# LN2 of the first two token blocks cut into single tiles, the table load moved to the start, and a new written order, in an adaLN + H3 convolution + SwiGLU kernel

## The chip, the cores and the metric

The kernel runs on one core of a Trainium2 chip. The time is the device time of one execution in microseconds (us). The kernel before takes 597.68 us, the median of three runs (597.65 to 598.74). A profiled execution of the same kernel took 598.64 us, with a span of 596.9 us in the trace; the rows quoted below are from that one. Engines: PE is the matmul engine (TensorE) and PEld its weight loads, DVE is VectorE, ACT is ScalarE, POOL is GpSimd, SP is the engine whose queue issues the transfers (DMA).

## The reference

```python
mod = (silu(c) @ w_mod).reshape(1, 6, 1, 512)     # sa, ca, ga, sb, cb, gb
h = layernorm(x) * (1 + ca) + sa                  # x: 2048 tokens x 512
k_shift = sum(shift(k, t) * shift_k[:, t])        # 4 taps, causal, per channel
kv = k_shift * v
y = irfft(rfft(kv, 4096) * rfft(ssm_k, 4096))[:2048] + kv * ssm_D
x = x + ga * (h * y)
h = layernorm(x) * (1 + cb) + sb                  # LN2
x = x + gb * ((silu(h @ w_gate) * (h @ w_up)) @ w_down)   # 512 -> 1792 -> 512
```

All of it is in fp32.

## The kernel before, in words

**The front** computes the convolution. The 512 channels are four blocks of 128, numbered 0 to 3 (c_ in the code). For each block the four taps (tap0, tap, L188 to 208) and the product with v (times_v, L211) run on DVE, ACT and POOL in the channel-major layout. The long convolution is a transform in two stages, written as matmuls: x_turn transposes kv on PE, x_first (L233) does the first stage of kv, k_first and k_turn (L253, L271) that of the filter ssm_k; skip (L1045) adds ssm_D to one row of the filter first. swap_x is a stream transpose in place on DVE. The second stage works on half blocks n = 0 to 7 (n // 2 is the block): x3 (L350) makes two of three linear forms of X on PE and copies them out (tile xs), x_sum adds these for the third, product3 (L359) multiplies with the filter's form straight from PSUM (pk) on DVE, and inv3 (L363) turns the three products back on PE, with copies into X on ACT. X0, X1 and X2 are then written to memory (put, tile away) and read back transposed in four transfers (get); X3 is transposed by DVE straight from PSUM (inv3s, L372).

**The gate and LN1.** The 2048 tokens are four blocks t of 512 (128 partitions times 4 token groups i). do_stats, gate_n (L521) and gate_p (L532, two tensor operations per token group with the broadcast modulation bcs) make the factor s that multiplies the convolution's result; each call says on which engine. y_pe (L539) does the last inverse step on PE from the X of two channel blocks, and y_into (L557) multiplies by s, adds to x and takes the statistics for LN2; y_gate and add_y (L551, L567) do the same in two steps. The modulation itself comes from three loads of w_mod (tile wm): mod_mul on ACT, mod_part on POOL or DVE, mod_bc and mod_T on PE, mod_mix on DVE.

**LN2 and the FFN.** The FFN is computed with fp32 split into a high and a low part, three matmuls for one product (PASSES, L774). Token blocks 0 and 1 are the first pair. For each of them: statistics and the power −0.5 on POOL (stats, L444, tile rsb), normalisation of the four token groups (norm2b, L578, tile n, alternating ACT and DVE), transposition into four channel tiles b on PE (norm_t, L594, tile nt, by halves h of two tiles), scale and shift on ACT (norm_s, L602, tile hraw), and the split of a half into high part by ACT (op_hi, L644) and low part by DVE or POOL (op_lo, L651). These are the operands B11, B21 (block 0) and B12, B22 (block 1). The gate and up products of the first two of 14 column blocks f are plain (gu_pe, L849, tile g); from f = 2 on, seven products in place of eight are used (gate_up_first, L911, whose first product is tile a; then gate_up), and the down products (tile dn) are fed in between. That part runs to the end and is the longest.

**What sets the order.** All engines are wrapped (InOrder, L32 to 40), so each one's instructions stand in the order in which the program's text calls them, and every row of the trace has line 40. The text of the front, from load_kh on, is a list of such calls in an order written out by hand. The table SLOTS (L54) gives the buffer for each allocation of five kinds of tile in turn: e8, r4, b16 and k2 in SBUF and ps, four double banks of PSUM. A tile that takes a buffer waits until the last reader of the former one is done. SP issues transfers in its own order too, so a load whose buffer is not free holds up those behind it. warm (L123) and warm_wide (L130) are matmuls without use to the result that are put where PE would wait.

Of the kernel before, what the change touches and what calls it, by code (L numbers as in the profile page):

```python
# [43 lines left out]
def adaln_h3_swiglu(ctx, tc, q, kT, vT, small, ssm, dskip, wgu, wdn, wmod, e_fwd, e_inv, w_c, out):  # L44
# [10 lines left out]
        "e8": "201345670143567013504312312341324314324314324314372154273124572134275124",  # L55
        "ps": "0123012301230123012310231023102310231023102310231023102310231231230123023102310231023102312031203120312031203120312031220310130101023122213021",
        "r4": "0123410231420312130413201401231230124012341023402130423014320413201432041342102314301204134210",
        "b16": "011234514354405234",
        "k2": "012102102010212010212010212010212010212010212021012021012021012021012021012021012021",
# [70 lines left out]
    def warm_wide():  # L130

        t = fp.tile([P, 2, 512], F32, tag="xs", name="wide", bufs=2)
        dve.memset(t, 1.0)
        t = t.bitcast(F32R)
        o = banks("wide")
        for _ in range(6):
            pe.matmul(o[:, 0], t[:, 0, 0:P], t[:, 1], start=True, stop=True)
        for w in (512, 256):
            for _ in range(8):
                for a in range(2):  # L140
                    pe.matmul(o[:, a, 0:w], t[rows(a), 0, 0:P], t[rows(a), 1, 0:w], start=True, stop=True)
# [8 lines left out]
    dve.memset(mhalf, -0.5)  # L150

# [14 lines left out]
    def load_small():  # L166
        sp.dma_start(sm, small)
# [276 lines left out]
    def stats(xs, name, done=False, rows_=range(TB)):  # L444
# [13 lines left out]
        if name in ("b0", "b1"):  # L458
            dve.tensor_scalar(rs[:, 0, :], v, EPS, None, op0=ALU.add)
            pool.tensor_tensor(rs[:, 0, :], rs[:, 0, :], mhalf, op=ALU.pow)  # L460
            dve.scalar_tensor_tensor(rs[:, 1, :], m, -1.0, rs[:, 0, :], op0=ALU.mult, op1=ALU.mult)
            return rs
# [139 lines left out]
    def norm_s(t, h):  # L602

        if not raw_h:
            raw_h.append(b16("hraw", (P, 2, NB, 512)))
        for k, pt in enumerate(NT.pop((t, h))):
            b = 2 * h + k
            act.activation(
                raw_h[0][:, t % 2, b], pt, AF.Identity, scale=modT[:, 1, b : b + 1], bias=modT[:, 0, b : b + 1]
            )  # L610
# [238 lines left out]
    def gu_pe(f, t, h):  # L849

        if h == 0:
            GU[f, t] = two("g")
        for b in (2 * h, 2 * h + 1):
            x = BOP[f"B{b // 2 + 1}{t + 1}"]
            for u in range(2):
                for n, (wa, xa) in enumerate(PASSES):
                    pe.matmul(
                        GU[f, t][u], WG[f][:, wa, u, b, :], x[:, xa, b % 2],
                        start=(b == n == 0), stop=(b == NB - 1 and n == 2),
                    )  # L860
# [169 lines left out]
    csil = cp.tile([P, 8], F32, name="csil")  # L1030
# [40 lines left out]
    def do_norm2a(t):  # L1071
        rs[t] = norm2a(t, True)
# [3 lines left out]

    load_kh(0, 0)
    load_small()
    tap0h(0, 0, e=dve)
    warm(16)  # L1080
    warm_wide()
    load_kh(0, 1)
    load_e(2)
    tap0h(0, 1, e=act)
    taph(0, 1, 0)
    load_ssm(0, 0)
    warm(3)
    load_dskip()
    load_ssm(0, 2)
    taph(0, 1, 1)  # L1090
    tap(0, 2)
    load_v(0)
    tap(0, 3)
    load_e(1)
    load_ssm(0, 1)
    skip(0)
    load_k(1)
    times_v(0, 3, e=dve)
    k_first(0, 2, e=act)
    k_first(0, 1, e=act)  # L1100
    times_v(0, 2, e=dve)
    x_turn(0, 1, e=act)
    times_v(0, 0, e=dve)
    times_v(0, 1, e=dve)
    x_turn(0, 0, e=act)
    load_ssm(0, 3)
    load_e(3)
    k_first(0, 3, e=act)
    load_e(0)
    x_first(0, 0, e=act)  # L1110
    k_first(0, 0, e=act)
    tap0(1, e=dve)
    tap(1, 1)
    tap(1, 2)
    tap(1, 3)
    load_ssm(1)
    skip(1)
    x_first(0, 1, e=act)
    swap_x(1)
    k_turn(0, 0, e=act)  # L1120
    k_turn(0, 3, e=act)
    load_wc()
    load_v(1)
    times_v(1, 1, e=pool)
    k_turn(0, 1, e=act)
    swap_x(3)
    load_k(2)
    load_ssm(2)
    k_first(1, 3, e=dve)
    tap0(2, e=act)  # L1130
    times_v(1, 0, e=pool)
    times_v(1, 2, e=pool)
    k_turn(0, 2, e=act)
    x_turn(1, 0, e=act)
    tap(2, 1)
    swap_x(0)
    load_v(2)
    tap(2, 2)
    k_first(1, 0, e=act)
    k_first(1, 1, e=act)  # L1140
    k_first(1, 2, e=act)
    room()
    skip(2)
    times_v(1, 3, e=pool)
    x_turn(1, 1, e=act)
    swap_x(2)
    silu_c()
    tap(2, 3)
    times_v(2, 1, e=pool)
    times_v(2, 2, e=pool)  # L1150
    x_first(1, 0, e=act)
    x_first(1, 1, e=act)
    swap_x(6)
    swap_x(7)
    x3(0, 2, e=act)
    k_turn(1, 0, e=act)
    x3(0, 1, e=act)
    load_x(2)
    times_v(2, 0, e=pool)
    x3(1, 2, e=act)  # L1160
    x3(1, 1, e=act)
    k_turn(1, 2, e=act)
    k_turn(1, 3, e=dve)
    do_stats(2, 0)
    load_x(1)
    x_sum(0, e=pool)
    mod_load(0)
    mod_mul(0, 1, e=act)
    mod_part(0, 1, e=pool)
    k_turn(1, 1, e=act)  # L1170
    k_first(2, 0, e=act)
    k_first(2, 2, e=act)
    x_sum(1, e=pool)
    k_first(2, 3, e=act)
    swap_x(4)
    x_turn(2, 0, e=act)
    product3(0, 0)
    product3(0, 1)
    product3(0, 2)
    mod_load(1)  # L1180
    mod_mul(0, 0, e=act)
    times_v(2, 3, e=pool)
    product3(1, 2)
    load_k(3)
    load_v(3)
    tap0(3, e=act)
    mod_part(0, 0, e=pool)
    product3(1, 1)
    do_stats(1, 0)
    inv3(0, e=act)  # L1190
    product3(1, 0)
    mod_mul(1, 1, e=act)
    x_turn(2, 1, e=act)
    x3(3, 2, e=act)
    mod_part(0, 2, e=pool)
    inv3(1, e=act)
    tap(3, 1)
    mod_part(0, 3, e=dve)
    tap(3, 2)
    tap(3, 3)  # L1200
    times_v(3, 3, e=pool)
    swap_x(5)
    x_first(2, 0, e=act)
    x_first(2, 1, e=act)
    swap_x(10)
    times_v(3, 0, e=pool)
    load_x(0)
    load_x(3)
    load_w(0)
    mod_part(1, 1, e=pool)  # L1210
    k_first(2, 1, e=act)
    x3(3, 1, e=act)
    do_stats(0, 0)
    swap_x(11)
    x_sum(3, e=pool)
    put(0)
    product3(3, 0)
    x3(2, 2, e=act)
    x3(2, 1, e=act)
    k_turn(2, 0, e=act)  # L1220
    k_turn(2, 2, e=act)
    k_turn(2, 3, e=act)
    x_sum(2, e=pool)
    product3(3, 1)
    times_v(3, 2, e=pool)
    times_v(3, 1, e=pool)
    product3(2, 0)
    product3(2, 2)
    w8_hi(0)
    product3(2, 1)  # L1230
    w8_lo(0, e=pool)
    mod_mul(1, 0, e=act)
    do_stats(3, 0)
    mod_part(1, 0, e=pool)
    mod_part(1, 2, e=pool)
    product3(3, 2)
    mod_part(1, 3, e=pool)
    do_stats(3, 1)
    k_turn(2, 1, e=act)
    x3(5, 1, e=act)  # L1240
    inv3(2, e=act)
    inv3(3, e=act)
    swap_x(9)
    do_stats(0, 1)
    load_ssm(3)
    skip(3)
    x_turn(3, 0, e=act)
    do_stats(1, 1)
    x_turn(3, 1, e=act)
    do_stats(2, 1)  # L1250
    swap_x(8)
    mod_bc(1)
    mod_bc(0)
    mod_mix()
    gate_n(2, 0, e=dve)
    x_first(3, 0, e=act)
    x_first(3, 1, e=act)
    swap_x(14)
    k_first(3, 1, e=act)
    get(0)  # L1260
    k_first(3, 2, e=act)
    k_first(3, 3, e=act)
    k_first(3, 0, e=act)
    x3(5, 2, e=dve)
    x_sum(5, e=dve)
    x3(4, 2, e=act)
    gate_p(2, 0, 1, e=pool)
    gate_p(2, 1, 1, e=pool)
    x3(4, 1, e=act)
    x_sum(4, e=pool)  # L1270
    gate_n(0, 0, e=act)
    gate_n(3, 0, e=act)
    put(1)
    product3(5, 0)
    product3(5, 2)
    gate_p(3, 0, 1, e=pool)
    product3(5, 1)
    load_einv()
    product3(4, 2)
    gate_n(0, 1, e=act)  # L1280
    gate_n(2, 1, e=act)
    gate_n(1, 0, e=act)
    product3(4, 0)
    product3(4, 1)
    get(1)
    inv3(5, e=act)
    inv3(4, e=act)
    swap_x(13)
    k_turn(3, 0, e=act)
    k_turn(3, 3, e=act)  # L1290
    swap_x(15)
    put(2)
    gate_p(3, 1, 1, e=pool)
    k_turn(3, 2, e=act)
    mod_load(2)
    gate_p(0, 0, 1, e=pool)
    gate_p(0, 3, 1, e=pool)
    k_turn(3, 1, e=act)
    x3(7, 2, e=act)
    swap_x(12)  # L1300
    get(2)
    x3(7, 1, e=act)
    gate_p(0, 1, 1, e=dve)
    x3(6, 1, e=act)
    gate_p(1, 0, 1, e=dve)
    gate_p(1, 1, 1, e=dve)
    x_sum(7, e=dve)
    x3(6, 2, e=act)
    product3(7, 1)
    gate_n(3, 1, e=act)  # L1310
    gate_n(1, 1, e=act)
    product3(7, 2)
    x_sum(6, e=pool)
    product3(7, 0)
    gate_p(0, 2, 1, e=pool)
# [276 lines left out]
```

## Time and profile before

| | us |
|---|---|
| median of three runs | 597.68 (597.65 to 598.74) |
| the profiled execution | 598.64 |
| its span in the trace | 596.9 |
| PE busy in the span | 578.0 (97%) |
| DVE busy | 464.3 (78%) |
| ACT busy | 305.4 (51%) |
| POOL busy | 304.1 (51%) |
| first plain product g starts | 165.43 |
| first of the seven products, a, starts | 195.78 |

The rows of the page and of the views are shown with the prediction. A row of a timeline gives the start, the length and the engine of a group of instructions, then output and inputs; in brackets stands the idle time ahead of it and what ended it. A row of a group gives the busy time, the mean in ns of one instruction, and idle time with what ended it.

### The profile page before, as it was taken

To read this page: it belongs to the slowest core of one execution; us is meant where nothing else is said; L and a number is where in the kernel's file an instruction comes from. 1 tells how busy PE (TensorE), PEld (TensorE's weight loads), DVE (VectorE), ACT (ScalarE), POOL (GpSimd) and SP (SyncE) were. 2 spreads that over 40 slices of the span, in tenths; PEclk is the share of its full clock that TensorE was granted. 3 is DMA by queue.
4 is the path that set the end of the run, shared out by engine and by line. 5 is a ranking of instruction groups with operands and counts; after the bars stand their busy time and mean duration, and the time that the engine had idled before them with its cause. 6 is when DMAs were issued, how large, how long until landed. Compare 5 with 4: busy or idle time off the path is not lost.

```text
span 596.9 us, 10541 instructions
## 1 busy us (share of the span) xinstructions
PE 578.0 (97%) x4250; PEld 465.4 (78%) x4250; DVE 464.3 (78%) x610; ACT 305.4 (51%) x466; POOL 304.1 (51%) x255
## 2 busy tenths in 40 slices
PE   9899999997799999999999999999999999999997
PEld 8875557436687777888888888888888888888885
DVE  5999999998789966666567776867676777687765
ACT  1899979961374444555544445524333333333430
POOL 0119498969457375656737574624333343424210
PEclk9999999999799999999999999999999999999999
DMA  8986489997024175353555451164343434343403
GB/s 298 385 348 253 151 281 288 236 299 164 2 71 154 41 257 200 122 177 132 188 204 185 158 211 54 55 228 177 123 159 124 158 125 159 124 160 125 158 2 141
DMA packets 32611, 102.59 MB, mean 172 GB/s; under 512 B 2353, under 2 KB 14769, under 8 KB 26802
## 3 DMA queue, kind: packets, MB, share of 16 engines
q1 hardware_dynamic: 32562, 101.92, 49.4%
q8 instruction: 33, 0.54, 0.4%
q14 instruction: 16, 0.13, 0.1%
HBM read 69.40 MB, written 32.51 MB: 171 GB/s over the span
## 4 chain that ended last, share of the span: by engine, by line
PE 79%; DVE 11%; DMA 5%; ACT 2%; issue 1%; SPq 1%; POOL 0%; ACTq 0%; DVEq 0%
PE a L40 23%; PE dn L40 14%; PE c L40 12%; PE b L40 6%; PE da L40 6%; DVE u L40 3%; PE dc L40 3%; PE iv L40 3%; PE pk L40 3%; PE s L40 2%; DMA X<-away 2%; DMA away<-X 2%; DVE X L40 1%; PE db L40 1%; PE px L40 1%
## 5 line engine op out<-in xcount | busy, mean ns | idle before, releaser
L40 PE MATMUL a<-op,wsum 128*128 128x512 f32 x432 | 110.8, 392 | 0.7 <-ACT r L40 0.7
L40 PE MATMUL dn<-wd,acts 128*128 128x512 f32 x360 | 91.0, 391 | 1.1 <-DVE sg L40 0.8
L40 PEld LDWEIGHTS a<-op,wsum 128*128 128x128 f32 x432 | 78.7, 188 | 15.8 <-ACT r L40 1.2
L40 PEld LDWEIGHTS dn<-wd,acts 128*128 128x128 f32 x360 | 67.1, 188 | 15.5 <-DVE sg L40 1.2
L40 ACT COPY p<-a 128x512 f32<-128x512 f32 x50 | 29.4, 588 | 65.8 <-PE a L40 65.7
L40 POOL TENSOR_TENSOR wa<-ws,wa 128x512 fp32r<-128x512 f32 (+1 forms) x28 | 32.4, 1178 | 48.2 <-ACT wa L40 48.2
L40 DVE TENSOR_TENSOR x<-x,dn 128x512 f32<-128x512 f32 x64 | 43.1, 681 | 16.5 <-PE dn L40 16.4
L40 ACT COPY r<-a 128x512 f32<-128x512 f32 x24 | 14.1, 587 | 58.5 <-PE a L40 58.5
L40 POOL TENSOR_TENSOR tb<-wds 128x256 f32<-128x256 f32 x12 | 8.9, 738 | 65.2 <-DVE wds L40 65.2
L40 PE MATMUL c<-op,wa 128*128 128x512 f32 x156 | 40.3, 394 | 0.0
L40 DVE TENSOR_TENSOR b<-r,c 128x512 f32<-128x512 f32 x24 | 16.6, 694 | 30.1 <-ACT sg L40 30.1
L40 PE MATMUL c<-op,wsum 128*128 128x512 f32 x156 | 39.6, 389 | 0.0
L40 POOL TENSOR_TENSOR vt<-u,vt 128x512 f32<-128x512 f32 x12 | 15.4, 1320 | 45.5 <-DVE u L40 37.9
L40 PE MATMUL b<-op,wa 128*128 128x512 f32 x144 | 36.9, 391 | 0.0
L40 DVE STREAM_TRANSPOSE X<-X 128x1024 f32<-128x1024 f32 x16 | 36.7, 2332 | 0.0
L40 POOL TENSOR_TENSOR s<-s,bcs 128x512 f32<-128x512 f32 x26 | 34.1, 1322 | 1.7 <-DVE s L40 0.7
L40 PEld LDWEIGHTS c<-op,wsum 128*128 128x128 f32 x156 | 29.3, 188 | 6.1
L40 DVE TENSOR_TENSOR x<-x,da 128x512 f32<-128x512 f32 x48 | 32.7, 682 | 1.2 <-PE da L40 1.1
L40 POOL TENSOR_TENSOR wsum<-sr,wsum 128x1024 fp32r<-128x1024 f32 x14 | 33.5, 2395 | 0.0
L40 POOL TENSOR_TENSOR wd<-wds,wd 128x1024 fp32r<-128x1024 f32 x7 | 17.3, 2468 | 31.0 <-ACT wd L40 31.0
L40 PEld LDWEIGHTS c<-op,wa 128*128 128x128 f32 x156 | 28.2, 188 | 6.1 <-DVE b L40 0.9
L40 PEld LDWEIGHTS b<-op,wa 128*128 128x128 f32 x144 | 26.3, 188 | 4.9
(174 smaller groups left out, 1366.5 us busy)
## 6 DMA issues: line engine op xcount, KB each, us to landing
ds<-wsum SPq DMA_DIRECT2D x12, 1024.0 KB, 7.5
wsum<-ds SPq DMA_DIRECT2D x12, 1024.0 KB, 6.4
dw<-wa SPq DMA_DIRECT2D x12, 768.0 KB, 5.6
wa<-dw SPq DMA_DIRECT2D x12, 768.0 KB, 4.3
ws<-in_wgu SPq DMA_DIRECT2D x16, 512.0 KB, 4.1
wds<-in_wdn SPq DMA_DIRECT2D x14, 512.0 KB, 7.2
wm<-in_wmod SPq DMA_DIRECT2D x3, 2048.0 KB, 13.0
away<-X SPq DMA_DIRECT2D x3, 2048.0 KB, 10.7
```

What stands on the lines that cost most here:

```text
L40: return lambda *a, **k: self.tc.keep_in_program_order(f(*a, **k))
```

## The change: what it does

1. warm_wide is gone. In its place stand more of the small identity matmuls: 47 ahead of the first use of PE, 11 ahead of the first group of y, and 11 behind the second.
2. The tile csil is allocated early, and a Silu of a constant is written into it as ACT's first work. ACT's table load belongs to it, and so stands ahead of all data. A load of the small inputs goes first on SP.
3. LN2 of token blocks 0 and 1: the statistics are three calls (rs1, rs2, rs3), the normalisation is one call for each token group (norm1; block 0 all on ACT, block 1 one on DVE and three on ACT), and norm_t, norm_s, the splits (hi1, lo1) and gu_pe work on one channel tile b in place of a half of two. The number of products is the same. lo1 of tiles 0 and 1 of B11 and of tile 0 of B21 are on POOL, the rest on DVE.
4. The order of the front is new throughout, and so is SLOTS. Among it: x_sum of half blocks 0 and 3 on DVE (both were on POOL) and of 5 on POOL (was DVE); one mod_part from DVE to POOL; gate_n(2,0) and x3(5,2) from DVE to ACT; gate_p on DVE is that of (2,0), (1,2), (3,3), (3,2) in place of (0,1), (1,0), (1,1); k_turn(0,1) and k_first(3,2) on DVE in place of k_turn(1,3) and k_first(1,3); load_w(1) ahead of put(2).

The core of the diff, with "..." for what is left out:

```diff
-    def warm_wide():
...
+    csil = cp.tile([P, 8], F32, name="csil")
+    act.activation(csil[:, 0:TB], mhalf, AF.Silu)
...
-    def norm_t(t, h):
-
-        NT[t, h] = two("nt")
-        for k, pt in enumerate(NT[t, h]):
-            b = 2 * h + k
-            for i in range(4):
-                pe.transpose(pt[:, i * P : (i + 1) * P], nrm[t, i // 2][:, i % 2, b * P : (b + 1) * P], ident)
+    def norm_t(t, b):
+
+        if b % 2 == 0:
+            NT[t, b // 2] = two("nt")
+        pt = NT[t, b // 2][b % 2]
+        for i in range(4):
+            pe.transpose(pt[:, i * P : (i + 1) * P], nrm[t, i // 2][:, i % 2, b * P : (b + 1) * P], ident)
...
+    def hi1(n, k, e=act):
+        if k == 0:
+            BOP[n] = free.pop(0)
+        copy(e, BOP[n][:, 0, k], h_raw(n)[:, k])
+
+    def lo1(n, k, e=dve):
+        o = BOP[n]
+        e.tensor_tensor(o[:, 1, k], h_raw(n)[:, k], o[:, 0, k].bitcast(F32), op=ALU.subtract)
...
-    def gu_pe(f, t, h):
+    def gu_pe(f, t, b):
...
+    def rs2(t):
+        pool.tensor_tensor(rs[t][:, 0, :], rs[t][:, 0, :], mhalf, op=ALU.pow)
...
+    def norm1(t, i, e=act):
...
+        if e is act:
+            act.activation(n, x, AF.Identity, scale=r[:, 0, i : i + 1], bias=r[:, 1, i : i + 1])
+        else:
+            dve.tensor_scalar(n, x, mvs[t][:, 2 * i : 2 * i + 1], r[:, 0, i : i + 1], op0=ALU.subtract, op1=ALU.mult)
```

At the start of the program the first rows of ACT before are these (u is the tap's sum, kt at first the k input and then the filter's form, s a PSUM tile, x a transposed half):

```order
L40 ACT_TABLE_LOAD
L40 ACTIVATE u_87<-kt_84,sm 128x1024
L40 COPY kt_178<-s_179 128x4x4x32 x2
L40 COPY kt_178<-s_190 128x4x4x32 x2
L40 COPY x_211<-kvt 128x1024
```

and these now:

```order
L40 ACT_TABLE_LOAD
L40 ACTIVATE csil<-mhalf 128x4
L40 ACTIVATE u_88<-kt_86,sm 128x1024
L40 COPY kt_163<-s_164 128x4x4x32 x2
L40 COPY kt_163<-s_175 128x4x4x32 x2
L40 COPY x_199<-kvt 128x1024
```

The table load now belongs to an instruction that needs no transfer, where it belonged to the scaling of u.

On SP, the loads of the middle of the front stood like this before (ss is ssm_k of a channel block, and ss_339 that of block 2; x is a token block of q):

```order
L40 DMA kt_337<-in_kT 128x2048
L40 DMA ss_339<-in_ssm 128x2048
L40 DMA vt_380<-in_vT 128x2048
L40 DMA x_511<-in_q 128x2048
L40 DMA x_563<-in_q 128x2048
L40 DMA wm<-in_wmod 128x4096 x2
```

and stand like this now (ss_796 is that of block 3, ss_825 that of block 2):

```order
L40 DMA vt_402<-in_vT 128x2048
L40 DMA kt_502<-in_kT 128x2048
L40 DMA vt_504<-in_vT 128x2048
L40 DMA x_666<-in_q 128x2048
L40 DMA x_713<-in_q 128x2048
L40 DMA ss_796<-in_ssm 128x2048
L40 DMA ss_825<-in_ssm 128x2048
L40 DMA away_831<-X_246 128x4096
```

The filter of block 2 moved from ahead of the v of block 2 to behind the filter of block 3 and just ahead of put(0).

On POOL, around LN2 of block 0, before (wm and part are the modulation, rsb the factor of LN2 with its power, s with bcs a gate_p, op a low part, wg a weight's low part):

```order
L40 TENSOR_TENSOR rsb_1824<-rsb_1824,mhalf 128x4
L40 TENSOR_TENSOR part_1830<-wm 128x512
L40 TENSOR_TENSOR s_1182<-s_1182,bcs 128x512 x2
L40 TENSOR_TENSOR op<-hraw,op 128x1024
L40 TENSOR_TENSOR wg<-ws,wg 128x1024
L40 TENSOR_TENSOR rsb_2013<-rsb_2013,mhalf 128x4
```

and now:

```order
L40 TENSOR_TENSOR part_1759<-wm 128x512
L40 TENSOR_TENSOR s_974<-s_974,bcs 128x512 x2
L40 TENSOR_TENSOR rsb_1827<-rsb_1827,mhalf 128x4
L40 TENSOR_TENSOR s_1277<-s_1277,bcs 128x512 x2
L40 TENSOR_TENSOR wg<-ws,wg 128x1024
L40 TENSOR_TENSOR op<-hraw,op 128x512 x2
L40 TENSOR_TENSOR x_713<-x_713,s_974 128x4x256
L40 TENSOR_TENSOR op<-hraw,op 128x512
L40 TENSOR_TENSOR rsb_1980<-rsb_1980,mhalf 128x4
```

The part and one gate_p went ahead of the first power; an addition and three small low parts took the place of one large one between the powers. On PE, the same place before, from the last y (n_0 and n_1 are the normalised token groups, two rows to a transposed tile nt):

```order
L40 MATMUL y<-X_240,ei 64x128 x8
L40 MATMUL y<-X_435,ei 64x128 x8
L40 MATMUL nt<-ident,n_0_1863 128x128 x2
L40 MATMUL nt<-ident,n_1_1895 128x128 x2
L40 MATMUL nt<-ident,n_0_1863 128x128 x2
L40 MATMUL nt<-ident,n_1_1895 128x128 x2
L40 MATMUL g<-op,wg 128x512 x24
L40 MATMUL nt<-ident,n_0_2017 128x128 x2
L40 MATMUL nt<-ident,n_1_2020 128x128 x2
```

and now:

```order
L40 MATMUL y<-X_246,ei 64x128 x8
L40 MATMUL y<-X_416,ei 64x128 x8
L40 MATMUL nt<-ident,n_0_1866 128x128 x2
L40 MATMUL nt<-ident,n_1_1901 128x128 x2
L40 MATMUL nt<-ident,n_0_1866 128x128 x2
L40 MATMUL nt<-ident,n_1_1901 128x128 x2
L40 MATMUL g<-op,wg 128x512 x36
L40 MATMUL nt<-ident,n_0_2031 128x128 x2
L40 MATMUL nt<-ident,n_1_2034 128x128 x2
```

Thirty-six products of block 0 now stand ahead of the first transposed tile of block 1, where 24 did; all four tiles of block 1 follow each other, where 12 more products stood between the second and the third.

More of the change, by code (lines that the diff above doesn't have):

```diff
@@ L1196, in adaln_h3_swiglu @@
-    inv3(1, e=act)
+    x3(3, 1, e=act)
+    load_ssm(3)
     tap(3, 1)
-    mod_part(0, 3, e=dve)
+    swap_x(4)
+    x3(2, 1, e=act)
+    skip(3)
+    x3(2, 2, e=act)
+    x_sum(2, e=pool)
+    load_ssm(2)
+    skip(2)
     tap(3, 2)
     tap(3, 3)
+    times_v(3, 2, e=pool)
+    put(0)
+    mod_bc(0)
     times_v(3, 3, e=pool)
-    swap_x(5)
-    x_first(2, 0, e=act)
-    x_first(2, 1, e=act)
-    swap_x(10)
-    times_v(3, 0, e=pool)
+    x_sum(3, e=dve)
+    load_w(0)
+    k_first(2, 0, e=act)
@@ L1414, in adaln_h3_swiglu @@
-    gu_act(0, 1)
-    gu_end(0, 1)
+    gate_p(1, 1, 1, e=pool)
+    y_into(1, 0, 1)
+    norm_s(0, 1, e=act)
+    hi1("B11", 1, e=act)
+    w8_lo(1, e=pool)
+    lo1("B11", 0, e=pool)
+    norm_t(0, 2)
+    norm_t(0, 3)
+    load_wd(1)
+    lo1("B11", 1, e=pool)
+    y_into(1, 2, 3)
+    rs1(1)
+    acts_room()
+    norm_s(0, 3, e=act)
+    gu_pe(1, 0, 0)
+    gu_pe(1, 0, 1)
+    y_gate(2, 0, 1)
+    add_y(2, 0, 4, (2, 3), e=pool)
+    norm_s(0, 2, e=act)
+    hi1("B21", 0, e=act)
+    room()
@@ new lines, in adaln_h3_swiglu @@
+    gu_pe(0, 0, 0)
+    lo1("B21", 0, e=pool)
+    rs2(1)
+    gu_pe(0, 0, 1)
+    hi1("B21", 1, e=act)
+    gu_pe(1, 0, 2)
+    gu_pe(0, 0, 2)
+    rs3(1)
+    norm1(1, 0, e=dve)
+    norm1(1, 1, e=act)
+    norm1(1, 2, e=act)
+    norm1(1, 3, e=act)
+    norm_t(1, 0)
+    add_y(3, 0, 4, (0, 1), e=dve)
+    norm_t(1, 2)
+    norm_t(1, 1)
+    norm_s(1, 0, e=act)
+    hi1("B12", 0, e=act)
+    norm_s(1, 1, e=act)
+    load_w(2)
+    norm_s(1, 2, e=act)
+    add_y(2, 0, 4, (0, 1), e=dve)
+    lo1("B21", 1, e=dve)
@@ L1424, in adaln_h3_swiglu @@
     room()
-    load_w(3)
     def norm_stats(t, rows_):
```

548 lines of the change are left out of this document (264 added, 284 removed).

## The prediction

> **What bounds the kernel now.** I read the page first (busy shares, chain of work that ended last), then the busy time by stretches, then the chain in order of time, and then the timeline of each engine around 7, 100, 115, 150 and 190 us.
>
> ```profile
> PE 578.0 (97%) x4250; PEld 465.4 (78%) x4250; DVE 464.3 (78%) x610; ACT 305.4 (51%) x466; POOL 304.1 (51%) x255
> PE 79%; DVE 11%; DMA 5%; ACT 2%; issue 1%; SPq 1%; POOL 0%; ACTq 0%; DVEq 0%
> ...
> 10.00:111.30 101.30, 98.36 (x1436) 65.95 (x1440) 100.19 (x95) 90.21 (x119) 61.38 (x48) 1.00 0.84 286
> 111.30:151.30 40.00, 34.92 (x554) 22.38 (x538) 36.57 (x50) 19.06 (x25) 32.47 (x24) 1.00 0.90 225
> 151.30:165.20 13.90, 10.27 (x97) 9.65 (x97) 11.97 (x20) 4.95 (x6) 6.58 (x5) 0.75 0.01 2
> 165.20:195.80 30.60, 29.57 (x140) 24.04 (x137) 27.49 (x38) 18.23 (x25) 18.02 (x13) 1.00 0.37 129
> 195.80:596.90 401.10, 396.20 (x1988) 335.52 (x1988) 285.11 (x406) 170.48 (x291) 184.95 (x162) 1.00 0.39 145
> ```
>
> A row of stretches reads: start and end, length, then the busy time of PE, weight loads, DVE, ACT and POOL, the granted clock, and the DMA's share and rate. The 97% of PE on the page is an average that hides the stage that matters. From 195.8 on, PE works 396.20 of 401.10 us, and this part of the program is not edited: every microsecond by which its first product, the tile called a, starts earlier is one off the end. Ahead of it, PE is busy but not what ends the waits. From 10 to 111.3 us DVE works 100.19 of 101.30: it is the bound there, with 1.1 us of idle time. From 111.3 to 151.3 the chain is a round trip of X2 through memory. From 151.3 to 165.2 almost nothing useful happens on PE (the clock granted falls to 0.75): the LN2 of block 0 runs through ACT, PE, ACT and POOL one after the other.
>
> ```profile
> 113.81 1.95 ACT X L40 x2
> 115.77 9.02 DMA away<-X
> 125.78 5.30 SPq L40
> 131.12 11.21 DMA X<-away
> ...
> 165.43 5.47 PE g L40 x24
> ...
> 195.78 1.63 PE a L40 x6
> ```
>
> These are rows of the chain in order of time: start, length, what. The first plain product g begins at 165.43 and a at 195.78. The forecast is therefore when a begins in the changed kernel.
>
> **The start.** Removed: the wide products. Moved: the table load, from behind the second half of kt to ahead of all data.
>
> ```profile
> 7.48 1.28 ACT L40 ACT_TABLE_LOAD   x1 [7.48 <-DMA kt<-in_kT]
> 8.78 1.15 ACT L40 ACTIVATE u<-kt,sm 128x1024 f32<-128x1024 f32 x1
> 9.96 6.06 DVE L40 SCALAR_TENSOR_TENSOR u<-kt,sm,u 128x1024 f32<-128x1024 f32 x3 [2.10 <-ACT u L40]
> 12.51 0.83 PE L40 MATMUL warm<-ident 128*128 128x128 f32 x6
> 13.27 2.41 PE L40 MATMUL s<-er,ss 64*128 64x128 f32 x32
> ```
>
> The half of kt lands at 7.48 in both kernels. Then the scaling of u starts at once instead of at 8.78, and DVE, which sat 2.10 us for it, starts 8.78 − 7.48 = 1.3 us earlier. The second load of the old kernel lies in a stretch where ACT works 90.21 of 101.30, so I count nothing for it. The 47 identity products that replace the wide ones are two records each; 94 × 0.83/6 = 13.0 us from about 1.3 would end near 14.3, and near 15.7 with the slower first ones. The first useful product began at 13.27, so PE comes up to 2.4 us late. DVE hides that: its taps and its products with v last until about 17 in either order. If that cover is gone, the cost is those 2.4.
>
> [...]
>
> **DVE up to the last product of block 2.** The new order gives DVE other work.
>
> ```profile
> 64.39 0.68 DVE L40 TENSOR_TENSOR part<-wm 128x512 f32<-128x512 f32 x1
> 98.48 1.00 DVE L40 TENSOR_SCALAR s<-x,rsa 128x512 f32<-128x512 f32 x2
> 101.63 1.25 DVE L40 COPY xs<-px 128x1024 f32<-128x1024 f32 x1
> 102.92 1.41 DVE L40 TENSOR_TENSOR xs<-xs 128x1024 f32<-128x1024 f32 x1
> 117.84 4.42 DVE L40 TENSOR_TENSOR s<-s,bcs 128x512 f32<-128x512 f32 x6
> ```
>
> Gone from it are one part (0.68), one gate_n (1.00) and one x3 copy (1.25): 2.93. New are two x_sum for one (net 1.41) and one gate_p, two instructions of 4.42/6 = 0.74: 2.89. The K and kt copies that it gives and takes cancel. So the balance is nil, and by work alone DVE would be done 1.3 (start) + 1.1 (idle time) = 2.4 us earlier. Against that stand waits that the old order doesn't have: mod_mix directly behind the broadcast's copy, product3(5,2) ahead of PE, and product3(4,0) third instead of fifth in its group, so that it waits for x_sum(4), which stands on POOL behind a gate_p. The trace does not show them. The lower bound is nothing; the upper one is a whole x_sum on POOL with a gate_p's two instructions ahead of it:
>
> ```profile
> 123.34 2.40 POOL L40 TENSOR_TENSOR xs<-xs 128x1024 f32<-128x1024 f32 x1 [5.01 <-ACT xs L40]
> L40 POOL TENSOR_TENSOR s<-s,bcs 128x512 f32<-128x512 f32 x26 | 34.1, 1322 | 1.7 <-DVE s L40 0.7
> ```
>
> 2.40 + 2 × 1.32 = 5.0. Following the rows through the new order I get about 3.3 in all (0.9, 0.9 and 1.5), which is in the middle. 3.3 − 2.4 = 0.9: the copies of inv3(4), which ended at 115.76, end near 116.7, and X2 is back near 143.2. New ahead of put(2) on SP is also load_w(1), 0.5 MB, at the stretch's 225 GB/s at most 2.3 us of the same DMA engines: 145.5. DVE comes to the y that reads X2 at 146.1 by my walk of its order, so neither is late; POOL comes last.
>
> **POOL up to the power of LN2(0).** Where the old kernel's power ran at 150.10 to 151.1, rows of the new order give it as the sum of what POOL has to do from x_sum(6) on.
>
> ```profile
> L40 POOL TENSOR_TENSOR wm<-wm 128x1024 f32<-128x1024 f32 x3 | 7.1, 2370 | 0.6 <-ACT wm L40 0.6
> 151.09 1.26 POOL L40 TENSOR_TENSOR part<-wm 128x512 f32<-128x512 f32 x1
> 150.10 1.02 POOL L40 TENSOR_TENSOR rsb<-rsb,mhalf 128x4 f32<-128x4 f32 x1 [1.25 <-DVE rsb L40]
> ```
>
> x_sum(6) starts with DVE's lateness at 123.34 + 0.9 = 124.2 and takes 2.40; six gate_p are 12 × 1.32 = 15.8; three wm sums 7.1; the part 1.26; the power 1.02. That ends at 151.8, **0.7 us later** than before.
>
> **LN2(0) by single tiles.** From the end of the power (151.1) to the first g (165.43) the old kernel needs 14.3 us.
>
> ```profile
> L40 ACT ACTIVATE n<-x,rsb 128x512 f32<-128x512 f32 x4 | 3.0, 808 | 16.0 <-DVE rsb L40 16.0
> 170.74 1.03 PE L40 MATMUL nt<-ident,n 128*128 128x128 f32 x8
> L40 ACT ACTIVATE hraw<-nt,modT 128x512 f32<-128x512 f32 x8 | 5.8, 775 | 9.2 <-PE nt L40 9.2
> L40 ACT CAST acts<-sg 128x512 fp32r<-128x512 f32 x4 | 2.4, 619 | 3.9 <-DVE sg L40 3.9
> 162.17 2.36 POOL L40 TENSOR_TENSOR op<-hraw,op 128x1024 fp32r<-128x1024 f32 x1 [7.24 <-ACT op L40]
> ```
>
> In the new one, the small product on DVE is 0.2, four normalisations on ACT 4 × 0.81 = 3.2, two transposed tiles 1.0, one hraw 0.8, one cast of 512 columns 0.6, and half of the 2.36 of the low part on POOL, 1.2: 7.0, with handovers of about 0.1 four times 7.4. POOL has one gate_p (2.6) and the low part of a weight (2.4) to do meanwhile; 151.8 + 5.0 = 156.8 lies ahead of its operand at about 157.8, so they are hidden with 1 us to spare. One y group on PE lies beside it. First g: 151.8 + 7.4 = 159.2 against 165.43. Term: 7.4 − 14.3 = **−6.9**. Where an operand has landed, single tiles mean more, smaller instructions, and no product is added.
>
> **From the first g to a.** Before: 195.78 − 165.43 = 30.4 us. Of that, 96 g products at 5.47/24 = 0.228 are 21.9, 24 dn at about the same duration 5.5, the two pairs of transposed tiles of block 1 2.1: 29.5, so waits are 0.9. After, PE issues norm_t(1,3) with no product left ahead of it, and that tile lies in the two-bank buffer that norm_s(1,2) reads. PE stands until ACT has done three norm_s and a cast, 3 × 0.775 + 0.62 = 2.9, less 1.0 for the two transposed tiles ahead: 1.9, and all products of the fourth tile of block 0 and of block 1 stand behind it. Without it the wait is nothing. I add what is new of it, with the old waits partly gone: **+1.1**, to 31.5.
>
> **Sum.** 0.7 − 6.9 + 1.1 = −5.1. For conflicts of DVE and POOL that I have not placed I allow 1.0 (nothing to 2.6, one gate_p, being the bounds), so −4.1. The profiled execution took 598.64, 1.74 beyond its span; it would take 594.5. The median of the runs is 0.96 below the profiled one, so the forecast is 593.6, with a starting near 191.7.
>
> **Rivals.**
>
> *The front gains too.* If none of the 3.3 us of new waits comes true, DVE's 2.4 us pass through x_sum(6) to POOL's chain: −3.3, and by smaller handovers −3.5. For it: DVE is the bound and has only 1.1 of idle time. Against it: x_sum(4) stands behind a gate_p on POOL by the written order. It gives 590.1.
>
> *The gain is given back in the front.* The ssm_k of block 2 is now loaded near the end of the front's loads, behind that of block 3 on SP, whose buffer comes free with times_v(2,0) on POOL. I estimate its issue at 59.0, from the POOL rows. skip(2) on DVE stands ahead of tap(3,2), which ran at 65.00.
>
> ```profile
> 65.00 4.73 DVE L40 SCALAR_TENSOR_TENSOR u<-kt,sm,u 128x2046 f32<-128x2046 f32 x2
> 27.00 4.67 DMA vt<-in_vT
> ss<-in_ssm SPq DMA_DIRECT2D x3, 1024.0 KB, 10.0
> ```
>
> With 4.67 us, as vt took, it lands at 63.7 and costs nothing; with the median of 10.0 of the ss loads it lands at 69.0 and DVE stands 4.0. That gives 593.6 + 4.0 = 597.6, no change. It decides from a landing of 6.0 us.
>
> *Slower: POOL is slowed by DVE.* Between the power of LN2(0) and the low part of B21 POOL now has eight instructions in a row (two of gate_p, the weight, two low parts, an addition, a low part, the next power), all in line with PE's g. The same instruction of POOL takes two lengths:
>
> ```profile
> 174.35 0.73 POOL L40 TENSOR_TENSOR sr<-sr,ws 128x256 f32<-128x256 f32 x1
> 175.04 1.72 POOL L40 TENSOR_TENSOR sr<-ws 128x256 f32<-128x256 f32 x1
> 183.87 2.32 DVE L40 TENSOR_TENSOR op<-hraw,op 128x1024 fp32r<-128x1024 f32 x1
> ```
>
> The sr sums take 0.73 or 1.72, and DVE's own low part, with two operands in SBUF as well, took 2.32 here, where its tile of 1024 took 1.41 as an x_sum. At +1.0 each, 8 less 1.5 of cover (the 1 us to spare and the handovers) = 6.5 us are lost, which gives 600.1. It decides from 5.6/8 = 0.7 us each, where the 4.1 of gain are gone. Against it: the 26 gate_p have a mean of 1.322 with DVE busy beside them, and DVE's work there is mostly y, with an operand in PSUM. [...]
>
> **How the numbers follow.** My own case 0.50, the front gains too 0.14, given back 0.12, slowed POOL 0.24. About 0.2% (1.2 us) is what a measurement of this kernel can tell from no change. Own range: 593.6 − 4.1 = 589.5 (no allowance 1.0, no lateness of POOL 0.7, no new wait of PE 1.1, and the 1.3 of the start passing through) to 593.6 + 3.4 = 597.0 (the 2.4 of the start's cover and the 1.0 to spare on POOL both lost). Faster: 0.48 of the own case, 0.14, and 0.04 of the third: 0.66. Same: 0.02 and 0.06: 0.08. Slower: 0.24 and 0.02: 0.26. The whole range takes in the first two and most of the slowed POOL: 589.0 to 600.5.
>
> **What would show it.** The first scaling of u at 7.5 and DVE's taps at 8.7; the copies of inv3(4) ending near 116.7; the power of LN2(0) ending near 151.8; four n on ACT, and g at 159.2; a gap of nearly 2 us on PE ahead of the last transposed tile of block 1; a near 191.7; the rest 401 us long. Wrong would be: DVE standing at skip(2) for ss near 65; gate_p or low parts on POOL longer than 2 us; DVE or POOL reaching the power later than 153; or a rest of other length.

## The result, and the profile after

The changed kernel is **slower**: 602.02 us, the median of 13 runs (600.39 to 604.19), beside 598.97 for the kernel before in as many (597.65 to 602.1). The ratio is 1.0048, with a 95% interval of 1.0032 to 1.0064. Forecast was 593.6, 0.7% less than the 597.68 it was set beside; the kernel before, in 13 runs, turned out 1.3 us slower than those three. The profiled execution took 600.88 with a span of 599.1.

The busy shares on the page of the changed kernel:

```profile
PE 582.9 (97%) x4286; PEld 469.0 (78%) x4286; DVE 462.3 (77%) x607; ACT 308.6 (52%) x475; POOL 305.2 (51%) x256
```

They hardly differ from those of before. Its busy time by the same stretches:

```profile
10.00:111.30 101.30, 97.85 (x1410) 65.63 (x1417) 99.42 (x91) 90.43 (x119) 60.19 (x45) 1.00 0.91 294
111.30:151.30 40.00, 39.90 (x605) 25.95 (x589) 38.73 (x51) 21.12 (x27) 34.10 (x25) 1.00 0.76 197
151.30:165.20 13.90, 13.28 (x121) 11.36 (x120) 13.38 (x31) 8.22 (x12) 12.05 (x9) 1.00 0.13 40
165.20:195.80 30.60, 25.64 (x115) 20.85 (x113) 23.49 (x26) 15.69 (x24) 11.04 (x9) 0.94 0.16 50
195.80:599.10 403.30, 397.61 (x1988) 336.53 (x1988) 283.64 (x406) 170.48 (x291) 187.14 (x166) 1.00 0.40 149
```

The stretch from 151.3 to 165.2, in which PE was busy for 10.27 of 13.90 us before, at a mean clock of 0.75, is filled: 13.28 us, at a mean clock of 1.00. The loss is in the next one. From 165.2 to 195.8 PE works 25.64 of 30.60, where it worked 29.57. The timeline of PE shows where, first of before, then of after:

```profile
165.18 5.72 PE L40 MATMUL g<-op,wg 128*128 128x512 f32 x24
170.74 1.03 PE L40 MATMUL nt<-ident,n 128*128 128x128 f32 x8
171.53 2.99 PE L40 MATMUL g<-op,wg 128*128 128x512 f32 x12
174.36 1.04 PE L40 MATMUL nt<-ident,n 128*128 128x128 f32 x8
175.15 13.86 PE L40 MATMUL g<-op,wg 128*128 128x512 f32 x60
188.85 2.88 PE L40 MATMUL dn<-wd,acts 128*128 128x512 f32 x12
192.56 3.02 PE L40 MATMUL dn<-wd,acts 128*128 128x512 f32 x12 [0.83 <-DVE sg L40]
195.78 1.63 PE L40 MATMUL a<-op,wa 128*128 128x512 f32 x6 [0.20 <-issue]
197.24 1.54 PE L40 MATMUL b<-op,wsum 128*128 128x512 f32 x6
```

```profile
162.79 5.61 PE L40 MATMUL g<-op,wg 128*128 128x512 f32 x24
168.23 1.52 PE L40 MATMUL nt<-ident,n 128*128 128x128 f32 x12
172.63 1.11 PE L40 MATMUL nt<-ident,n 128*128 128x128 f32 x4 [2.87 <-ACT hraw L40]
173.39 14.87 PE L40 MATMUL g<-op,wg 128*128 128x512 f32 x60
188.10 5.60 PE L40 MATMUL dn<-wd,acts 128*128 128x512 f32 x24
196.64 2.90 PE L40 MATMUL a<-op,wa 128*128 128x512 f32 x6 [2.94 <-POOL sr L40]
199.34 1.62 PE L40 MATMUL b<-op,wsum 128*128 128x512 f32 x6
```

(The second begins with the last 24 of the first 36 g; the first 12 start at 159.94.) The first g comes 165.18 − 159.94 = 5.2 us earlier, dn only 188.85 − 188.10 = 0.8 us earlier, and b 199.34 − 197.24 = 2.1 us later. From b to the end of the span both take the same: 596.9 − 197.24 = 399.7 and 599.1 − 199.34 = 399.8. So 7.3 us are lost between the first g and b, at two waits of PE, 2.87 and 2.94 us, each with a slow stretch that sets in about half a microsecond before the wait ends: the clock granted by stretches of the changed kernel is

```profile
173.00:175.00 2.00, 2.00 (x8) 1.71 (x7) 1.97 (x4) 0.98 (x3) 1.04 (x2) 0.50 0.30 66
194.00:197.00 3.00, 0.36 (x1) 0.39 (x2) 3.00 (x4) 0.00 (x0) 2.92 (x4) 0.84 1.01 400
197.00:200.00 3.00, 3.00 (x9) 2.33 (x9) 1.66 (x3) 0.42 (x1) 1.11 (x2) 0.59 0.97 397
```

(the last three numbers are clock, DMA share and rate). The clock stands at 0.50 from 172.2 to 175.6 and from 196.1 to 199.3. So the 60 g behind the first wait take 14.87 instead of the 13.86 of before, the transposed tile ahead of them 0.76 from its start to theirs instead of 0.41 (172.95 to 173.36 in the run with the late tile, below), and the six of a 2.70 to the start of b instead of 1.46. 2.87 + 1.0 + 0.35 + 2.94 + 1.24 = 8.4, less the old waits of 0.83 and 0.20 that are gone: 7.4, which is the 7.3 within the small differences of the other rows.

### The profile page after: what moved, and what is told of

It reads as the page before. It is cut to its first block, busy times and chain, and to the rows that moved or that the text cites. A ratio compares the mean times of both kernels' runs of the same rounds, so it can differ in the third digit from the quotient of the medians.

```text
span 599.1 us, 10613 instructions
## 1 busy us (share of the span) xinstructions
PE 582.9 (97%) x4286; PEld 469.0 (78%) x4286; DVE 462.3 (77%) x607; ACT 308.6 (52%) x475; POOL 305.2 (51%) x256
## 4 chain that ended last, share of the span: by engine, by line
PE 82%; DVE 11%; DMA 3%; ACT 2%; issue 1%; POOL 1%; SPq 0%; DVEq 0%; ACTq 0%
PE a L40 23%; PE dn L40 14%; PE c L40 11%; PE b L40 6%; PE da L40 6%; PE g L40 4%; PE iv L40 3%; PE s L40 3%; PE dc L40 3%; DMA er<-in_e_fwd 3%; DVE u L40 2%; DVE X L40 2%; DVE xs L40 2%; PE kt L40 2%; PE pk L40 1%
## 5 line engine op out<-in xcount | busy, mean ns | idle before, releaser
L40 POOL TENSOR_TENSOR wa<-ws,wa 128x512 fp32r<-128x512 f32 (+1 forms) x28 | 30.9, 1127 | 53.1 <-ACT wa L40 53.1
L40 POOL TENSOR_TENSOR vt<-u,vt 128x512 f32<-128x512 f32 x12 | 17.0, 1440 | 38.6 <-DVE u L40 26.7
L40 POOL TENSOR_TENSOR s<-s,bcs 128x512 f32<-128x512 f32 x24 | 30.6, 1288 | 1.9 <-ACT s L40 1.0
L40 DVE SCALAR_TENSOR_TENSOR u<-kt,sm,u 128x2046 f32<-128x2046 f32 (+4 forms) x13 | 30.4, 2342 | 0.7 <-ACT u L40 0.4
```

The costliest lines, as they stand in the source:

```text
L40: return lambda *a, **k: self.tc.keep_in_program_order(f(*a, **k))
```

## The experiments

Ratios are to the kernel before, run on the same chip each time. As its own median differs between chips (598.97 to 600.38), marks in the profile (starts of the first g, of a, of b) are compared beside them. "Less than the changed kernel" is the difference of the spans of two single profiled executions; that of the changed kernel, 599.1, belongs to an execution 1.1 us below the median of its 13. By the ratios the differences are larger, each with about 1.4 us of uncertainty: 4.7 to 4.8 us for each of the first three experiments, 7.0 for both, 8.7 for all three and 10.9 with x_sum(2) moved.

The theory: the first g came as forecast, and the gain is lost at the two waits. The second wait is named in its row with POOL (sr), yet what the program makes a wait for is a release of its PSUM bank by the second add of a down product on DVE, and that add stands in DVE's queue behind a long diff. The rivals: that the wait is POOL's, as the row has it; that one wait only takes the other's place; that the front or POOL's slowness is the cause.

**The diff behind the adds.**

```diff
     gu_end(0, 1)
-    diff("B22", "B22", "B11", e=dve)
     downs(1)
...
     gu_end(1, 1)
+    diff("B22", "B22", "B11", e=dve)
```

> The changed kernel with only DVE's diff of B22 moved from ahead of the four adds of the down products to behind them. Theory (a waits for its PSUM bank, which the second of these adds releases, and the diff in front takes 3.4 us beside POOL's low part): the adds run as dn ends, a starts near 193.9 instead of 196.64 without a slow clock: 3 to 4 us less. Rival (a waits for POOL, as the wait's row names it, sr ending at 195.9): a starts where it did, within 0.5 us.

597.86 us, ratio 0.9968 (0.9949 to 0.9987), span 596.2, 2.9 less than the changed kernel. PE's rows and DVE's of this run:

```profile
188.91 5.60 PE L40 MATMUL dn<-wd,acts 128*128 128x512 f32 x24
194.35 1.52 PE L40 MATMUL a<-op,wa 128*128 128x512 f32 x6
```

```profile
192.76 2.48 DVE L40 TENSOR_TENSOR x<-x,dn 128x512 f32<-128x512 f32 x4
195.16 1.20 DVE L40 TENSOR_TENSOR acts<-sg,acts 128x512 fp32r<-128x512 f32 x1
196.28 1.76 DVE L40 TENSOR_TENSOR hraw<-hraw 128x1024 f32<-128x1024 f32 x1
```

No call on POOL was moved, and the wait at a is gone whole; the six products of a take 1.52 us, where they took 2.90. On POOL of this run the first sr only begins after a has begun, at 194.35:

```profile
195.07 0.74 POOL L40 TENSOR_TENSOR sr<-ws 128x256 f32<-128x256 f32 x1
```

So POOL's sr, named in the row, was not what a waited for; it only ended at about that time. The same part of DVE in the changed kernel shows what was in the way:

```profile
191.21 0.81 DVE L40 TENSOR_TENSOR acts<-sg,acts 128x512 fp32r<-128x512 f32 x1 [1.59 <-ACT acts L40]
191.95 3.40 DVE L40 TENSOR_TENSOR hraw<-hraw 128x1024 f32<-128x1024 f32 x1
195.26 2.47 DVE L40 TENSOR_TENSOR x<-x,dn 128x512 f32<-128x512 f32 x4
```

The second of the four adds ends near 196.5, and a starts at 196.64. In the kernel before, the same diff had run 13 us ahead of a (DVE's row of that kernel):

```profile
182.73 1.22 DVE L40 TENSOR_TENSOR hraw<-hraw 128x1024 f32<-128x1024 f32 x1
```

**The split earlier.** In the new order the split of the next weights is called behind the two last Silu of g, so ACT's casts for it stand behind a Silu that waits for PE's last products, and the casts of acts behind them. The first of these casts, which ran at 188.79 in the changed kernel, was this row of ACT in the kernel before:

```profile
182.64 0.92 ACT L40 CAST wa<-ws 128x512 fp32r<-128x512 f32 x2
```

```diff
+    split_w(2)
     gu_act(1, 1)
     op_lo("T3", e=dve)
     gu_pe(0, 1, 3)
     gu_act(0, 1)
-    split_w(2)
```

> The changed kernel with the split of the weights of f = 2 called where the old order had it, ahead of the two Silu of g of block 1. Theory (the gain of LN2 is lost again where the product a waits): ACT casts the weight near 182 to 185 instead of behind the last Silu at 188.8, POOL is done with its low parts before 191, the cast of acts runs right behind its Silu, and DVE's diff ahead of the adds of the down products is not stretched from 1.2 to 3.4 us. a then follows dn at once: 2.9 us of wait and 1.3 of slow clock go, so 4.2 us less than the changed kernel, 0.993 of it. Rival (the loss is in the front, and the last stage is limited by later work): within 1 us of the changed kernel.

597.94 us, ratio 0.9969 (0.9952 to 0.9987), span 595.2, 3.9 less than the changed kernel. POOL's low part of the wsum tile starts at 185.81, where it started at 191.44; DVE's diff takes 1.76 instead of 3.40, and a waits 0.93 and takes 1.62 instead of 2.90:

```profile
187.71 5.60 PE L40 MATMUL dn<-wd,acts 128*128 128x512 f32 x24
194.23 1.62 PE L40 MATMUL a<-op,wa 128*128 128x512 f32 x6 [0.93 <-POOL sr L40]
```

As expected but for that 0.93: the diff, from 191.17 on, then meets POOL's next sr, from 191.81 to 193.53.

**The last tile of block 1 later.**

```diff
-    norm_t(1, 3)
     gu_pe(0, 0, 3)
+    gu_pe(1, 0, 3)
+    norm_t(1, 3)
...
     gu_act(0, 0)
-    gu_pe(1, 0, 3)
```

> The changed kernel with the last transposed tile of block 1 on PE behind the products of the fourth tile of block 0 (12 products, 2.7 us) instead of ahead of them. Theory: the wait of 2.87 us on PE for hraw and the slow clock behind it (about 1 us) go, and dn starts 3 to 4 us earlier, near 184.5. But a still waits for the adds behind the split, which stand behind the last Silu on ACT; these move with g, so the end gains about the same, 3 to 4 us. Rival (PE is fed by DVE's low parts of block 1, which come no earlier): the wait turns up again at a later g, and the gain is under 1.5 us.

597.61 us, ratio 0.9969 (0.9949 to 0.9990), span 595.5, 3.6 less than the changed kernel. The 12 products run in place of the wait, and dn starts at 184.36 instead of 188.10:

```profile
168.54 1.53 PE L40 MATMUL nt<-ident,n 128*128 128x128 f32 x12
169.83 3.00 PE L40 MATMUL g<-op,wg 128*128 128x512 f32 x12
172.95 0.66 PE L40 MATMUL nt<-ident,n 128*128 128x128 f32 x4
173.36 11.16 PE L40 MATMUL g<-op,wg 128*128 128x512 f32 x48
184.36 5.60 PE L40 MATMUL dn<-wd,acts 128*128 128x512 f32 x24
192.91 1.62 PE L40 MATMUL a<-op,wa 128*128 128x512 f32 x6 [2.95 <-POOL sr L40]
```

The wait at a is still 2.95: the two are apart from each other. Here a took 1.62, and the products behind it were slow, b and c: b took 2.71 from 194.37 on and c 2.00, where the changed kernel's took 1.62 and 1.53.

**Both.**

> The changed kernel with both the early split and the late tile. Theory: both gains add up, 7 to 8 us less than the changed kernel and 4 to 5 less than the kernel before: a near 189. Rival (one wait merely takes the place of the other): no more than the larger of the two alone, 4 us less than the changed kernel.

595.38 us, ratio 0.9931 (0.9906 to 0.9957), span 593.3. That is 5.8 less than the changed kernel, where the two alone gave 3.9 and 3.6: less than their sum of 7.5, more than either, and so between the theory and its rival. 1.67 us of wait at a remain, behind a diff of 1.75.

**All three.** The diff is moved as well.

> The changed kernel with all three moves: early split, late tile, and the diff of B22 behind the adds of the down products. In the run with the first two a still stood 1.67 us for the adds behind a diff of 1.75 us. Theory: that wait goes, a starts near 190.7 and follows dn at once; 1.5 us less than with two moves, 7 to 8 less than the changed kernel, and faster than the kernel before by 4 to 5. Rival (POOL's low part of the weight, or another release, comes last then): a stays within 0.5 us of 192.4.

593.63 us, ratio 0.9902 (0.9880 to 0.9925), span 591.8, 7.3 less than the changed kernel:

```profile
184.70 5.69 PE L40 MATMUL dn<-wd,acts 128*128 128x512 f32 x24 [0.42 <-DVE wd L40]
190.40 1.62 PE L40 MATMUL a<-op,wa 128*128 128x512 f32 x6
```

The order's gain is now whole: a starts 5.4 us earlier than in the kernel before, and the first g came 5.2 earlier. Within each execution, from the first g to the dn behind the first a, b and c, it is 34.8 us in the kernel before, 42.2 in the changed kernel, 38.0 with the diff moved, 38.9 with the split, 38.5 with the tile, 36.2 with both and 34.6 with all three.

**Single tiles undone for the first operand.** The cast and the low part of B11 are made as one half of two tiles.

```diff
-    hi1("B11", 0, e=act)
...
-    hi1("B11", 1, e=act)
+    op_hi("B11")
     w8_lo(1, e=pool)
-    lo1("B11", 0, e=pool)
+    op_lo("B11", e=pool)
...
-    lo1("B11", 1, e=pool)
```

> The changed kernel with the first operand, B11, cast and subtracted as one half of two tiles again (one cast on ACT behind both hraw, one low part of 2.4 us on POOL), all else by single tiles. Theory: the first g waits for both hraw (ends near 158.8), a cast of 1.05 and a low part of 2.36, and starts near 162.3 instead of 159.94; the delay of 2.2 us is passed on to a and the end. Rival (the gain at the first g comes from the order alone, the normalisation on ACT and y behind it, and single tiles add nothing): g starts within 0.5 us of 159.94.

604.69 us, ratio 1.0086 (1.0061 to 1.0111), span 602.8. The g group goes on at 162.68, after a wait of 1.90 for POOL's op (one record before it is early), and a at 199.34, 2.7 later than in the changed kernel. In this run the power was already 0.35 later (151.51 for 151.16). So single tiles in the first operand alone bring about 2.4 of the 5.2 us (2.74 at g less the 0.35); the rest is left to the order and to the normalisation that is all on ACT, which no run took apart.

**The table load late again, and early in the kernel before.** In the changed kernel the early Silu is taken out:

```diff
     csil = cp.tile([P, 8], F32, name="csil")
-    act.activation(csil[:, 0:TB], mhalf, AF.Silu)
```

> The changed kernel without the early Silu of a constant, so that the table load again stands in front of the scaling of u (the tile csil is written later as before, nothing else differs). Theory (DVE bounds the front, so its start is passed on whole): DVE's taps start 1.3 us later, the copies of inv3(4) end 1.3 later than 117.06, and the first g comes 1.3 later than 159.94; the end 1.3 later. Rival (the start is absorbed by waits for data in the front): the taps start later, but the copies of inv3(4) end within 0.4 us of 117.06.

603.51 us, ratio 1.0064 (1.0042 to 1.0087), span 601.6. DVE's taps start at 9.46 instead of 8.63 (kt landed earlier in this run: the tap's first step starts at 5.72 instead of 6.16), the copies of inv3(4) end at 117.56 instead of 117.06, and the first g comes at 161.33, 1.4 later. Between the theory and its rival: 0.5 of 0.8 is passed on through the front. The other 0.9 at the first g is PE's pace at y: the last 20 of 32 products, from 154.76 on, took 2.35 us, where the changed kernel's 32 took 1.97 at a clock of 1.00. The interval of the ratio overlaps that of the changed kernel, so the time itself shows no difference. And in the kernel before, the same two lines are put in at the start:

> The kernel before with only the table load moved to the start by a Silu of a constant into csil. Theory: DVE's taps start 1.3 us earlier, near 8.65, and the copies of inv3(4) end near 114.5; the round trip of X2 and so the end move by the same 1.3, to 0.998 of the kernel before. Rival (DMA or PE's wide products set the first stage): the copies of inv3(4) end within 0.4 us of 115.75 and the time doesn't change.

597.61 us, ratio 0.9965 (0.9944 to 0.9985). DVE's taps start at 8.76 instead of 9.96, the copies of inv3(4) end at 114.41 instead of 115.75, 1.3 earlier as expected. The gain in time, 0.35%, is 2 us (0.9 to 3.4), and the expected 1.3 lies within that. The changed kernel, with the same early Silu, has one table load, at 0.72, where the kernel before has a second at 36.98. The profiled execution, at 594.85 the fastest of its 12, has a at 192.09, 3.7 earlier. Its rows give the parts: the power of LN2(0) starts at 148.09 instead of 150.10, 2.0 earlier; the 64 products of y ahead of the first g take 4.24 instead of 5.42 (in the kernel before the clock was 0.50 for the first 3.5 us of them, up to 162.5); and dn waits 0.29 instead of 0.83.

**Where the front lost.** The new order begins its taps 1.3 us earlier than the old one and ends inv3(4) 1.3 later. In every profiled execution of it up to here, POOL's x_sum(2) fell beside DVE's tap(3,3) or x_sum(3), and one of these was 2.0 to 2.2 us longer. DVE and POOL of the changed kernel, where it was the tap (the second of two):

```profile
66.40 6.83 DVE L40 SCALAR_TENSOR_TENSOR u<-kt,sm,u 128x2046 f32<-128x2046 f32 x2
73.15 1.21 DVE L40 TENSOR_TENSOR xs<-xs 128x1024 f32<-128x1024 f32 x1
```

```profile
68.72 2.36 POOL L40 TENSOR_TENSOR xs<-xs 128x1024 f32<-128x1024 f32 x1 [3.93 <-ACT xs L40]
```

Two taps took 4.73 in the kernel before (the row at 65.00 above). The move, on top of the three:

```diff
-    x_sum(2, e=pool)
...
     times_v(3, 2, e=pool)
+    x_sum(2, e=pool)
```

> The version with the three moves, and in the front x_sum(2) on POOL one place later, behind times_v(3,2), so that it no longer runs beside DVE's tap(3,3) and x_sum(3), which read two SBUF tiles each. In all runs of the new order so far one of these two took 2.2 us longer than alone (4.5 for 2.3, or 3.4 for 1.2) while POOL's x_sum ran from about 68.7. Theory (DVE and POOL shut each other out there, and DVE bounds the front): both take their own time, the copies of inv3(4) end 2.2 us earlier, near 115.0 instead of 117.2, the first g near 157.8 and a near 188.2; the end 2.2 less than with the three moves. Rival (the front is also held by another wait, PE or a transfer): DVE gains 2.2 near 72 us but the copies of inv3(4) end less than 0.7 earlier.

591.26 us, ratio 0.9866 (0.9841 to 0.9892), span 589.5. Both of DVE's take their own time, the copies of inv3(4) end at 114.82, and all later marks move with them (first g 157.68, a 188.06):

```profile
66.01 4.72 DVE L40 SCALAR_TENSOR_TENSOR u<-kt,sm,u 128x2046 f32<-128x2046 f32 x2
70.64 1.22 DVE L40 TENSOR_TENSOR xs<-xs 128x1024 f32<-128x1024 f32 x1
```

2.3 us less than with three moves, where 2.2 were expected.

**The small product on POOL.** LN2's 128x4 product took 1.22 us on DVE beside POOL's gate_p at block 0.

```diff
     def rs2(t):
         pool.tensor_tensor(rs[t][:, 0, :], rs[t][:, 0, :], mhalf, op=ALU.pow)
+        pool.tensor_tensor(rs[t][:, 1, :], rs[t][:, 1, :], rs[t][:, 0, :], op=ALU.mult)
```

> The version before with one more move: the product of LN2's factor and the mean, 128x4, stands on POOL right behind the power (the mean is negated on DVE ahead of it), where DVE's took 1.22 us beside POOL's gate_p at block 0 and 0.16 alone at block 1. Theory (the small product is shut out by POOL, and it lies on the path to the first g): the normalisation on ACT starts 1.0 us earlier after the power than before (153.52 behind 152.18 in the changed kernel), and the first g and the end come 0.8 to 1.0 earlier. Rival (ACT then waits for modT or PE for y, so nothing is gained): the first g stays within 0.3 us relative to the power.

591.53 us, ratio 0.9867 (0.9839 to 0.9895), the same as without. From the start of the power to the first g it is 157.27 − 149.45 = 7.8 us, where the version before took 157.68 − 148.89 = 8.8: the 1.0 is there. But in this run the front was 0.5 later (a wait of 0.67 at skip(2), of which more below), and the time cannot tell the rest. It is not shown to be worth anything in time.

The fastest version is the one with x_sum(2) moved: 1.3% below the kernel before.

## Why the prediction was wrong

**The step that failed is "From the first g to a"**, which I put at +1.1, 31.5 us in all. It was 36.7 to the start of a, and the loss to b was 7.3. Two things in it were wrong.

- The wait for the last tile of block 1 was named, with its place and its queue, and mis-sized: 1.9 forecast, 2.87 measured. I took the two transposed tiles ahead of it as cover; but ACT began its three norm_s only when all three tiles were done, at 169.80, so nothing of the chain (0.78 + 0.62 + 1.44 = 2.84) was covered. Nor did I count the slow clock behind the wait, 1.4 with the transposed tile.
- The move of the split behind the two last Silu was not counted at all, nor that of the diff to just ahead of the adds. The split is a moved step of which each instruction had to be followed through each queue: the casts on ACT, behind them the cast of acts, behind that DVE's low part, then the diff, which now meets POOL's low part, then the adds that release the bank of a. The cost, 2.94 of wait and 1.2 of slow clock, is the larger part of the miss, and undoing either move took most of it away: 2.9 (the diff alone) and 3.9 (the split).

From the first g as measured, 159.94 + 31.5 = 191.4; with 1.0 more of the first wait, 1.4 of slow clock and 2.9 of the second wait it is 196.7, and a started at 196.64. Without the two waits it came at 190.40.

The other steps, one by one:

- **The start: right.** The scaling of u started at 7.45 and DVE's taps at 8.63. The identity products took 12.45 us, and the first useful product came at 13.72, 0.45 late and hidden.
- **DVE up to the last product: right in size by luck, wrong in cause.** The copies of inv3(4) ended at 117.06, forecast 116.7. But of the three new waits that I had named, of 0.9, 0.9 and 1.5, only 0.26 at product3(5,2) showed up. In their place stood a collision with POOL of 2.2 us that I had not looked for in the front (shown by its removal), and 0.67 at skip(2).
- **POOL up to the power: right.** It ended at 152.18, forecast 151.8.
- **LN2(0) by single tiles: right.** From the power's end to the first g 7.8 us, forecast 7.4; the small product on DVE took 1.22 where I had put 0.2. The trace of the kernel before had shown that 1.22 already, at 151.15 beside POOL's part.
- **The rest of the program: right**, 399.8 us from b on, as before.
- **From the profiled execution to the median: wrong.** I took 0.96 off for it; the 13 runs of the kernel before had their median 0.33 above its profiled execution, and the changed kernel 1.14 above.

Of the rivals, *the gain is given back in the front* had the right mechanism at a small price: the load of block 2's filter was issued near 59, as estimated, landed 7.1 us later, and skip(2) waited 0.67 for it in the changed kernel (its row names PE, but the transfer landed at 66.15 and skip(2) began at 66.19) and up to 1.35 in another run. That was one of the signs of being wrong that I had named. *Slower: POOL is slowed by DVE* came out near the right time, 600.1, for the wrong reason. Its eight instructions, which follow the power in these rows of POOL of the changed kernel, were not stretched:

```profile
151.16 1.02 POOL L40 TENSOR_TENSOR rsb<-rsb,mhalf 128x4 f32<-128x4 f32 x1
152.15 2.62 POOL L40 TENSOR_TENSOR s<-s,bcs 128x512 f32<-128x512 f32 x2
154.73 2.37 POOL L40 TENSOR_TENSOR wg<-ws,wg 128x1024 fp32r<-128x1024 f32 x1
158.81 2.63 POOL L40 TENSOR_TENSOR op<-hraw,op 128x512 fp32r<-128x512 f32 x2 [1.71 <-ACT op L40]
161.39 2.41 POOL L40 TENSOR_TENSOR x<-x,s 128x1024 f32<-128x1024 f32 x1
163.76 1.30 POOL L40 TENSOR_TENSOR op<-hraw,op 128x512 fp32r<-128x512 f32 x1
165.02 1.02 POOL L40 TENSOR_TENSOR rsb<-rsb,mhalf 128x4 f32<-128x4 f32 x1
```

The collision of the two engines is real, but it struck DVE, at other places: at the diff ahead of a (3.40 for 1.22 in the kernel before), at the tap (2.1 more), at the small product (1.22 for 0.16). The rows of the tap show both ways: the one that began at 68.77 beside an x_sum that had begun at 68.72 took 4.46, a little under the sum of the 2.36 of the x_sum and the 2.33 that a tap takes in the kernel before; and in the run with all three moves, where the tap began first, near 68.8 (the second of two that took 4.72 from 66.44), POOL's x_sum, from 69.30 on, took 4.09 instead of 2.36.

## What to carry to other kernels

When work is cut into smaller pieces so that an engine starts earlier, follow the same engine to the next place where it must wait: here 5.2 us were won at the first product and 7.3 lost within the 40 us behind it, at two waits that the order of other calls made. A wait that is named with one engine is tested by moving the other candidates one at a time; a moved call is priced by every queue that its instructions stand in, down to the one that frees a buffer. Before placing a POOL operation, look which DVE operation stands beside it: the four that were stretched here all read two tiles in SBUF (the diff and an x_sum, 3.40 for 1.22 each, the tap, 4.46 for 2.33, and the small product, 1.22 for 0.16).

## What the runs showed of the hardware

- In the changed kernel PE waited 2.87 us, to 172.63, and 2.94, to 196.64. The granted clock stood at 0.50 from 172.2 to 175.6 and from 196.1 to 199.3, at a cost of 1.4 and 1.2 us. In five of the experiments PE waited seven more times, for 2.87 to 2.95, and the products that followed took 1.4 to 1.7 us longer than without such a wait, each time; so a wait of three microseconds costs more than four here. The clock stayed at 1.00 after the waits of 2.40 (the kernel before, at 142.47) and 2.11 (the changed kernel, at 77.82), and the products of a were not slow after those of 1.67 (both moves, 1.60 us) and 0.93 (the split, 1.62).
- The length of a single wait doesn't settle it: in the kernel before, the clock was 0.50 from 155.7 to 162.5, behind two waits of 1.72 and 1.46 and through a third of 1.07. In two runs of the new order (the diff, the tile) the 32 products of y behind a wait of 0.25 and 16 products of one column each took 2.94 and 3.26 us, where those of the changed kernel, behind the same, took 1.97 at a clock of 1.00. What sets it is open.
- The table load, at the start with no data to wait for, took 1.28 us, and the next ACTIVATE started at 2.01, 1.29 after the load's start at 0.72. It is the same at the two loads of the kernel before: 7.48 and the next ACTIVATE at 8.78, and, right behind a copy, 36.98 and 38.27.
- DVE's product of 128x4 took 1.22 us at block 0, with POOL at work on a 128x512 tile, and 0.16 at block 1, with POOL idle: in the changed kernel the first ran from 152.21 to 153.43, and POOL's instruction beside it from 152.15 to 153.41.
